# A first unit in a computed order, and later units with scores, transposes and value products at one place each

## The chip, the core and the metric

One core of a Trainium2 chip. The metric is device time in microseconds of one launch. Time before: 814.76 us, the median of 3 runs (812.94 to 815.05).

## The reference

Three stages in a chain, all in float32:

```python
scores = scale * q @ k.T                 # (4, 8, 576, 64): batch, heads, sequence, dim
# heads 0-3: keep 0 <= rel < 32;  heads 4-7: keep 0 <= rel < 128 and rel % 4 == 0
attn = exp(scores - max) / (sum + 1e-9)  # masked scores are -1e9
x = (attn @ v)  -> (2304 tokens, 512)
h = maximum(maximum(x @ w1, x @ w2), x @ w3);  x = h @ w_out           # 768 wide
h = x @ w_in;  g = P3(h) / (1 + |b0||h| + |b1|h*h + 1e-6);  out = g @ w_out   # 2048 wide
```

## The kernel before

**Tiling.** The 2304 tokens are cut into 12 chunks of 192; two chunks make a unit of 384 tokens, and there are 6 units. Per chunk the attention of the plain heads ("p") and of the dilated heads ("d", regrouped so that each residue modulo 4 is a dense band) goes through steps that have letters in the code: S (scores on TensorE, with the mask added by a TensorE matmul for chunks 0 to 3 and by VectorE after them), MX (row maximum, VectorE), E (exponentials, ScalarE; for chunks 0 to 3 one activation for each of 6 or 8 score blocks, with an accumulated sum, later one activation for all, with a subtraction before and a sum after it on VectorE), SB (division by the sum, VectorE), X (transposes on TensorE in two halves, each copied to SBUF), V (value products on TensorE) and VE (the split of the result into a rounded high part x1h on ScalarE and a remainder x1l on VectorE, both float32r).

**Split products.** Each product of the two later stages is three float32r matmuls (high by high, high by low, low by high), in the helper `mm3`, lines 494 to 499.

**The stage after attention** is `moe1(u)`: 18 groups h(f, j) of 12 matmuls of 384 columns (6 blocks f, 3 weights j, the maximum over j on VectorE) and 4 groups x(c) of 18 such matmuls. The weights arrive as raw 64-bit words and are converted in the kernel, one step at a time: load (SP queue), abs (ScalarE), bits (two VectorE instructions), hi (ScalarE), lo (VectorE). There are 24 of these tiles (18 of w1, w2, w3 and 6 of w_out), and `moe1(0)` needs each just as it comes to its group; the 32 tiles of the third stage are converted during units 1 to 4 and spread out over 88 slots.

**What sets the order.** The first unit's attention (chunks 0 and 1) is written out by hand in the string START and runs in that order on every queue. From line 630 a loop over the units issues `moe1(u)` group by group, and after each group one row of the string UNIT (UNIT0 for the chunks 2 and 3), which holds the attention steps of unit u + 1. In that loop a planner puts the instructions of each engine in order by when it reckons them ready, with priority to what was issued earlier; TensorE's order follows the rows. The loads of q, k, v and weights are all on SP's queue; stores of x2d and w2d are on POOL's. TensorE runs dummy matmuls at "W" words so that it isn't idle (helper `busy`).

**PSUM** has 8 banks: mm (3), sc (2), tp (1), pv (2). In UNIT a chunk's S:p and S:d stand 3 rows (5 in the second chunk) apart, its four transposes stand in rows of their own, all through the one tp bank, and V and VE of the second chunk stand in row 22, after the last group of the unit.

**The third stage** is untouched by the change: 6 tiles of 384 tokens by 16 slices, from about 405 us to the end.

Of the kernel before, what the change touches and what calls it, by code (L numbers as in the profile page):

```python
# [64 lines left out]

UNIT = """
-
Sa:p
-
MXa:p Ea:p  # L70
SBa:p Sa:d MXa:d Ea:d Xa:p,1
Xa:p,0 SBa:d
-
-
Xa:d,1 Va:p Xa:d,0
Va:d
VEa:d
-
Sb:p VEa:p
-  # L80
-
MXb:p
-
Eb:p SBb:p Sb:d MXb:d Xb:p,1
Eb:d
Xb:p,0
SBb:d Xb:d,0
Xb:d,1 Vb:p Vb:d VEb:d VEb:p
# [4 lines left out]
def kernel(  # L93
    ctx: ExitStack,
    tc: tile.TileContext,
    masks: bass.AP,
# [10 lines left out]
    a_co: bass.AP,  # L107
    b_co: bass.AP,
# [30 lines left out]
    ACT_UNITS = 4  # L139
    MASK_PE = 4  # L140
    SC_AT = {(0, "p"): "pv", (1, "p"): "mm", (1, "d"): "pv"}
    QA = 2
    CVT = 4
# [5 lines left out]
    AHEAD = 1  # L149
# [38 lines left out]
    at_k = {}  # L188
    x1 = {}

    def load_k(b, part=None):

        if b not in at_k:
            at_k[b] = (
                at.tile([128, 2, S], F32, tag="kTp", bufs=2, name=f"kTp{b}"),
                at.tile([128, 8, S // 4], F32, tag="kTd", bufs=2, name=f"kTd{b}"),
            )
        kTp, kTd = at_k[b]
        src = kp_in[b].rearrange("p (a t) -> p a t", a=2)
        if part is None:  # L200
            nc.sync.dma_start(out=kTp, in_=src)
        elif part == 0:
            nc.sync.dma_start(out=kTp[:, :, 0:CH], in_=src[:, :, 0:CH])
            return
        else:
            nc.sync.dma_start(out=kTp[:, :, CH:S], in_=src[:, :, CH:S])
            return
        nc.sync.dma_start(out=kTd.rearrange("p n m -> p (n m)"), in_=kd_in[b])

    def load_q(c, g):  # L210
        if c >= NCH:
            return
        if g == "p":
            t = at.tile([128, 2 * BP, 2 * QP], F32, tag="qTp", bufs=QA, name=f"qTp{c}")
            nc.sync.dma_start(out=t.rearrange("p n w -> p (n w)"), in_=qp_in[c])
        else:
            t = at.tile([128, 8, 2 * M], F32, tag="qTd", bufs=QA, name=f"qTd{c}")
            nc.sync.dma_start(out=t.rearrange("p n w -> p (n w)"), in_=qd_in[c])
        at_raw[c, g] = t
# [8 lines left out]
    def load_v(c):  # L228
        ci = c % NC
        vp = at.tile([WP, BP, NP, D], F32, tag="vp", name=f"vp{c}")  # L230
        nc.sync.dma_start(out=vp.rearrange("p i h d -> p (i h d)"), in_=vp_in[c])
        nm = dil(ci)[1]
        vd = at.tile([WD, NP, 4 * D], F32, tag="vd", name=f"vd{c}")
        nc.sync.dma_start(out=vd[:nm].rearrange("p h e -> p (h e)"), in_=vd_in[c, 0:nm, :])
        at_raw[c, "v"] = (vp, vd)

    def attn_pieces(c):
# [12 lines left out]
        def SC(g):  # L250
# [6 lines left out]
            for j in range(2):  # L257
                at_bank = SC_AT.get((c, g), "sc")
                if at_bank != "sc":
                    t = (mm_p if at_bank == "mm" else pv_p).tile(  # L260
                        [128, 512], F32, tag=at_bank, name="sc")
                else:
                    t = sc_p.tile([128, 512], F32, tag="sc", bufs=2, name="sc")
# [11 lines left out]
            m16, m32 = (mP16, mP32) if plain else (mD16, mD32)  # L275
# [4 lines left out]
            for n in range(U):  # L280
                i, blk = divmod(n, BP)
                if plain:
                    k0 = key0(ci, blk)
                    lq, rk = qT[:, n, :], kTp[:, i, k0:k0 + WP]
                else:
                    lq, rk = qT[:, n, :], kTd[:, n, m0:m0 + nmk]
                nc.tensor.matmul(scs[n // G][:, n % G, :], lhsT=lq, rhs=rk,  # L287
                                 start=not pem, stop=not pem or n % G == G - 1)
            load_q(c + QA, g)
            if g == "d" and ci == 0 and b + 1 < B:  # L290
                load_k(b + 1)
            sb = at.tile([Q, U, WP if plain else WD], F32, tag="s" + g, bufs=SBB, name="sb")
            mx = at.tile([Q, U, 1], F32, tag="mx" + g, bufs=2, name="mx")
            sm = at.tile([Q, U, 1], F32, tag="sm" + g, bufs=2, name="sm")
            grp[g] = (sb[:, :, :W], Q, W, U, sm, mx, scs, mask(m32))

        def MX(g):
# [11 lines left out]
            if c < ACT_UNITS:  # L309
                nc.vector.tensor_scalar_mul(mx, mx, -SCALE)  # L310

        def E(g):
            sv, Q, W, U, sm, mx, scs, mk = grp[g]
            G = U // 2
            if c < ACT_UNITS:
                for n in range(U):
                    src = scs[n // G][:, n % G, :] if c < MASK_PE else sv[:, n]
                    nc.scalar.activation(out=sv[:, n], in_=src, func=AF.Exp, scale=SCALE,
                                         bias=mx[:, n], accum_out=sm[:, n])
            else:  # L320
                nc.vector.tensor_tensor(out=sv, in0=sv, in1=mx.to_broadcast([Q, U, W]),
                                        op=ALU.subtract)
# [3 lines left out]
        def SB(g):  # L326
# [3 lines left out]
            nc.vector.tensor_tensor(out=sv, in0=sv, in1=sm.to_broadcast([Q, U, W]), op=ALU.mult)  # L330

        def X(g, j, dve=False, bank="tp"):
            sv, Q, W, U = grp[g][:4]
            G = U // 2
            if bank == "tp":
                tp = tp_p.tile([128, TU], F32, tag="tp", name="tpp")
            else:
                tp = sc_p.tile([128, 512], F32, tag="sc", bufs=2, name="tpp")[:, 0:TU]
            tp = tp[:W].rearrange("w (n q) -> w n q", q=Q)
            pt = at.tile([WP, TU], F32, tag="pt", bufs=PT, name="pt")[:W].rearrange(  # L340
                "w (n q) -> w n q", q=Q)
# [8 lines left out]
        def V(g):  # L350
            vp, vd = at_raw[c, "v"]
            if c == 0:
                pv = mm_p.tile([128, 512], F32, tag="mm", name="pv")
            else:
                pv = pv_p.tile([128, 512], F32, tag="pv", name="pv")
            pv = pv[:, 0:TU].rearrange("p (a t) -> p a t", a=2)
            for a in range(2):
                pt = pts["p", a] if g == "p" else None
                for n in range(BP if g == "p" else 4):
                    for j in range(2):  # L360
# [6 lines left out]
                        else:  # L367
                            pt = pts["d", j]
                            nc.tensor.matmul(pv[rows, a, M * n:M * n + M],  # L369
                                             lhsT=vd[:nmk, 2 * a + j, D * n:D * n + D],  # L370
                                             rhs=pt[:, 2 * (n // 2) + a,
                                                    M * (n % 2):M * (n % 2) + M],
# [3 lines left out]
        def VE(g):  # L376
            pv = grp["v" + g]
            if g == "p":
                src, dh, dl = pv, x1h[:, 0:2, tok], x1l[:, 0:2, tok]
            else:  # L380
                src = pv.rearrange("p a (r m) -> p a r m", r=4)
                dh = x1h[:, 2:4, tok].rearrange("p a (m r) -> p a r m", r=4)
                dl = x1l[:, 2:4, tok].rearrange("p a (m r) -> p a r m", r=4)
            nc.scalar.activation(out=dh, in_=src, func=AF.Copy)  # L384
            nc.vector.tensor_sub(dl, src, dh.bitcast(F32))  # L385
            if g == "d" and 0 < c < NCH - 1:
                load_v(c + 1)

        return {"S": SC, "MX": MX, "E": E, "SB": SB, "X": X, "V": V, "VE": VE}
# [11 lines left out]
    done_words = set()  # L401

    def attn(u):

        for row in (UNIT0 if u == 1 else UNIT).strip().split("\n"):
            for word in row.replace("-", "").split():
                word = word.replace("a:", f"{2 * u}:").replace("b:", f"{2 * u + 1}:")
                if word not in done_words:
                    do(word)
# [36 lines left out]
    def cv_abs(i):  # L446
# [27 lines left out]
    def cv_lo(i):  # L474
# [4 lines left out]
        else:  # L479
            nc.vector.tensor_sub(slot[:, 512:1024], t, slot[:, 0:512].bitcast(F32))  # L480

    cv_at = {"load": 0, "abs": 0, "bits": 0, "hi": 0, "lo": 0}
    cv_steps = (("hi", cv_hi, "bits"), ("lo", cv_lo, "bits"), ("abs", cv_abs, "load"),
                ("bits", cv_bits, "abs"), ("load", cv_load, None))

# [15 lines left out]

    def moe1(u):
        x1h, x1l = x1[u]
        hs = {}
        for f in range(F1):
            for j in range(3):
                ps = mm_p.tile([128, 512], F32, tag="mm", name="mm")
                o = ps[:, 0:TU]
                w = w1s[f, j]
                mm3(o, [(w[:, 128 * c:128 * c + 128], w[:, 512 + 128 * c:640 + 128 * c],  # L510
                         x1h[:, c, :], x1l[:, c, :]) for c in range(KC)])
                if j == 0:
                    t = com.tile([128, TU], F32, tag="m", bufs=MB, name="m")
                    nc.scalar.activation(out=t, in_=o, func=AF.Copy)
# [390 lines left out]
```

## Time and profile before

| | |
|---|---|
| median of 3 runs | 814.76 us |
| the profiled execution | 815.14 us, span 813.4 us |
| granted TensorE clock, mean | 0.991 |
| TensorE matmul busy | 800.1 us, 98% of the span |
| VectorE, ScalarE, GpSimd busy | 614.1, 487.9, 39.2 us |
| chain that ended last | 96% TensorE |
| DMA | 82.54 MB |

Times are microseconds from the first instruction. A busy time is the union of an engine's instructions; a matmul's recorded time is longer than its pitch, since matmuls overlap, so costs on TensorE are read from starts. The chain of waits is followed back from the last instruction; each piece's time there is the time by which it moved the end.

### The profile page before, as it was taken

The page shows a single profiled execution, that of the slowest core. Times are in us where ns is not written, and L with a number is a line of the kernel's source. Part 1 is how long each engine was busy: PE and PEld are TensorE (multiplying, and loading weights), DVE is VectorE, ACT ScalarE, POOL GpSimd, SP SyncE. Part 2 cuts the span into 40 slices and gives each one's busy share as a digit, 9 for nine tenths or more (in the row PEclk, how much of TensorE's full clock was granted, in tenths as well). Part 3 has the DMA queues.
Part 4 walks back from the last instruction along what each step waited for, and adds up shares of the span by engine and source line. Part 5 has one row for each costly group of instructions (what it writes and reads, how often), then busy time and mean ns, then how long its engine had stood idle before and what let it go on. Part 6 is the DMA issues. An engine that isn't in the chain of part 4 may idle for free.

```text
span 813.4 us, 13081 instructions
## 1 busy us (share of the span) xinstructions
PE 800.1 (98%) x4965; PEld 745.1 (92%) x4965; DVE 614.1 (76%) x1184; ACT 487.9 (60%) x1023; POOL 39.2 (5%) x77
## 2 busy tenths in 40 slices
PE   7899999999999999999999999999999999999998
PEld 5699999999999999999998899999999999999996
DVE  2679755655656646637389899999999999998996
ACT  3578623333333334245398887787778778777775
POOL 0000000110111110000000000000000000000000
PEclk9799999999999999999999999999999999999999
DMA  8677435754554544328310011010002001001001
GB/s 267 245 263 271 159 106 171 228 167 158 171 175 161 178 163 149 107 101 272 120 63 1 1 39 40 1 42 37 1 1 79 1 0 40 1 1 38 2 1 39
DMA packets 29438, 82.54 MB, mean 101 GB/s; under 512 B 3904, under 2 KB 7488, under 8 KB 29376
## 3 DMA queue, kind: packets, MB, share of 16 engines
q1 hardware_dynamic: 24080, 64.66, 24.7%
q0 software_dynamic: 5296, 17.04, 5.5%
q8 instruction: 39, 0.64, 0.3%
q14 instruction: 23, 0.19, 0.1%
HBM read 63.87 MB, written 17.83 MB: 100 GB/s over the span
## 4 chain that ended last, share of the span: by engine, by line
PE 96%; ACT 1%; DVE 1%; DMA 1%; issue 0%; SPq 0%; POOL 0%; ACTq 0%
PE mm L498 12%; PE mm L497 12%; PE mm L499 12%; PE h L498 8%; PE acc L769 8%; PE h L499 8%; PE h L497 8%; PE acc L767 8%; PE acc L768 8%; PE sc L287 4%; PE tpp L343 2%; PE pv L369 2%; PE pv L363 1%; DMA mk<-in_masks_dram 1%; ACT x1h L384 1%; PE warmth L604 0%
## 5 line engine op out<-in xcount | busy, mean ns | idle before, releaser
L497 PE MATMUL mm<-x1h,w1s 128*128 128x384 f32 x432 | 147.7, 343 | 0.0
L498 PE MATMUL mm<-x1l,w1s 128*128 128x384 f32 x432 | 146.0, 338 | 1.0 <-DVE x1l L385 1.0
L499 PE MATMUL mm<-x1h,w1s 128*128 128x384 f32 x432 | 145.2, 336 | 0.0
L498 PE MATMUL h<-x2l,w2s 128*128 128x384 f32 x384 | 129.2, 337 | 0.0
L499 PE MATMUL h<-x2h,w2s 128*128 128x384 f32 x384 | 129.0, 336 | 0.0
L497 PE MATMUL h<-x2h,w2s 128*128 128x384 f32 x384 | 128.9, 336 | 0.0
L767 PE MATMUL acc<-w2s,gh 128*128 128x512 f32 x288 | 113.6, 395 | 0.0
L768 PE MATMUL acc<-w2s,gh 128*128 128x512 f32 x288 | 113.4, 394 | 0.0
L769 PE MATMUL acc<-w2s,gl 128*128 128x512 f32 x288 | 109.8, 395 | 0.0
L718 ACT ACTIVATE q<-h 128x384 f32<-128x384 f32 x96 | 47.2, 491 | 76.1 <-PE h L499 75.5
L498 PEld LDWEIGHTS mm<-x1l,w1s 128*128 128x128 f32 x432 | 81.6, 189 | 2.2 <-DVE x1l L385 2.2
L497 PEld LDWEIGHTS mm<-x1h,w1s 128*128 128x128 f32 x432 | 81.3, 189 | 0.6
L499 PEld LDWEIGHTS mm<-x1h,w1s 128*128 128x128 f32 x432 | 81.6, 189 | 0.0
L497 PEld LDWEIGHTS h<-x2h,w2s 128*128 128x128 f32 x384 | 72.1, 188 | 3.9
L498 PEld LDWEIGHTS h<-x2l,w2s 128*128 128x128 f32 x384 | 72.0, 188 | 3.8
L499 PEld LDWEIGHTS h<-x2h,w2s 128*128 128x128 f32 x384 | 72.1, 188 | 0.3
L516 DVE TENSOR_TENSOR m<-mm,m 128x384 f32<-128x384 f32 x72 | 39.9, 554 | 42.2 <-PE mm L499 41.4
L725 DVE SCALAR_TENSOR_TENSOR q<-q,cs,ab 128x384 f32<-128x384 f32 x96 | 59.1, 615 | 15.5 <-ACT ab L719 15.4
L720 ACT ACTIVATE p<-h,cs 128x384 f32<-128x384 f32 x96 | 65.1, 678 | 0.0
L769 PEld LDWEIGHTS acc<-w2s,gl 128*128 128x128 f32 x288 | 54.1, 188 | 11.9
L768 PEld LDWEIGHTS acc<-w2s,gh 128*128 128x128 f32 x288 | 54.1, 188 | 9.4
L767 PEld LDWEIGHTS acc<-w2s,gh 128*128 128x128 f32 x288 | 54.0, 188 | 9.0
(86 smaller groups left out, 1471.8 us busy)
## 6 DMA issues: line engine op xcount, KB each, us to landing
w1r<-in_w_dram SPq DMA_DIRECT2D x18, 512.0 KB, 6.6
raw<-in_w_in_dram SPq DMA_DIRECT2D x16, 512.0 KB, 4.0
w2d<-cvt POOLq DMA_DIRECT2D x32, 256.0 KB, 2.6
raw<-in_w_out_dram SPq DMA_DIRECT2D x16, 512.0 KB, 3.6
w2r<-w2d SPq DMA_DIRECT2D x32, 256.0 KB, 3.6
qTp<-in_qp_dram SPq DMA_DIRECT2D x12, 384.0 KB, 4.1
qTd<-in_qd_dram SPq DMA_DIRECT2D x12, 384.0 KB, 4.5
x2d<-xs POOLq DMA_DIRECT2D x24, 192.0 KB, 2.5
```

What stands on the lines that cost most here:

```text
L287: nc.tensor.matmul(scs[n // G][:, n % G, :], lhsT=lq, rhs=rk, start=not pem, stop=not pem or n % G == G - 1)
L343: nc.tensor.transpose(tp[:, i, :], sv[:, G * j + i, :], ident[:Q, :Q])
L497: nc.tensor.matmul(o, lhsT=lh, rhs=rh, start=(i == 0), stop=False)
L498: nc.tensor.matmul(o, lhsT=lh, rhs=rl, start=False, stop=False)
L499: pe_at[0] = nc.tensor.matmul(o, lhsT=ll, rhs=rh, start=False, stop=(i == n - 1))
L516: nc.vector.tensor_tensor(out=t, in0=o, in1=t, op=ALU.max)
L718: nc.scalar.activation(out=s["q"], in_=s["h"], func=AF.Square)
L720: nc.scalar.activation(out=s["p"], in_=s["h"], func=AF.Identity, scale=cs[:, 3:4], bias=cs[:, 2:3])
L725: nc.vector.scalar_tensor_tensor(out=s["q"], in0=s["q"], scalar=cs[:, 5:6], in1=s["ab"], op0=ALU.mult, op1=ALU.add)
L767: nc.tensor.matmul(o, lhsT=gh, rhs=w[:, 0:512], start=(c == 0), stop=False)
L768: nc.tensor.matmul(o, lhsT=gh, rhs=w[:, 512:1024], start=False, stop=False)
L769: nc.tensor.matmul(o, lhsT=gl, rhs=w[:, 0:512], start=False, stop=(c == F2 - 1))
```

## The change

1. START now holds the whole of units 0 and 1's attention (chunks 0 to 3), the conversion of all 24 weight tiles and the whole of `moe1(0)`, in one written order; the loop begins at u = 1. `moe1` is cut into pieces for it: H:k and P:k are the groups (the first three in two halves of 192 tokens, H as soon as chunk 0's part is there), M the evictions and maxima, HH and HL the split, Y and YS the x groups.
2. The masks come as bfloat16, with the identity and the coefficients in one load; the casts on POOL and VectorE go. The warm-up matmuls have 128 columns and are put in four times the W number ahead of the next bank's first work.
3. For chunks 0 to 3 the exponentials come in three kinds (A: as before; B: subtraction on VectorE, one activation, sum on VectorE; C: one activation per block, sum on VectorE), and the division may go to ScalarE.
4. In UNIT S:p and S:d of a chunk stand in one row, the four transposes in one row (banks tp, sc, sc, pv), V:p and V:d in one row, and V of the second chunk one group earlier.
5. The tokens in a block of 64 are put in another order (host side: q rows, masks, output), so that the split of the dilated part writes contiguously; the value products of d write in pieces of 16.
6. Loads of q, k and v for later chunks (q from chunk 4, k from batch 2, v from chunk 4) go on POOL's queue.

```diff
 START = """
-W:7
-...
+qp0 kp0 mk L W:19 S0:p,mm qd0 kd0 up MX0:p bits L E0:p qd1 hi W:10 S0:d,mm SM0:p L up lo
+SB0:p,act MX0:d W:1 S1:d,sc qp1 D0:d bits kp1 E0:d X0:p,0,mm up X0:p,1,mm SM0:d v0 XC0:p,0 MX1:d
+XC0:p,1 SB0:d W:3 S1:p,mm E1:d bits v1 X0:d,0,tp MX1:p V0:p,pv XC0:d,0 SB1:d hi X0:d,1,sc L
+VH0:p D1:p W:1 X1:d,1,pv XC0:d,1 X1:d,0,tp XC1:d,1 VL0:p V0:d,mm L E1:p lo XC1:d,0 SM1:p L up
+V1:d,pv SB1:p VH0:d up L VL0:d X1:p,0,mm VH1:d X1:p,1,sc bits XC1:p,0 H:0 L XC1:p,1 VL1:d hi
+bits V1:p,mm L hi H:1 lo VH1:p qp2 VL1:p up lo hi P:0 k1 bits up S2:p,sc M:0 bits hi lo hi H:2
+...
+MX3:p E3:p Y:0 VH3:d SM3:p SB3:p VL3:d X3:p,1,tp YS:0 Y:1 XC3:p,1 X3:p,0,sc YS:1 Y:2 XC3:p,0,dve
+V3:p,mm YS:2 Y:3 VH3:p VL3:p YS:3
 """
 UNIT = """
-...
+-
+Sa:p Sa:d,pv
+MXa:p MXa:d
+Ea:p
+Ea:d SBa:p
+SBa:d
+-
+-
+Xa:p,0 Xa:p,1,sc Xa:d,0,sc Xa:d,1,pv
+-
+Va:p Va:d
+VEa:p VEa:d
+Sb:p Sb:d,pv
+MXb:p MXb:d
+Eb:p
+Eb:d SBb:p
+SBb:d
+-
+Xb:p,0 Xb:p,1,sc Xb:d,0,sc Xb:d,1,pv
+-
+Vb:p Vb:d
+VEb:p VEb:d
 """
+    EXPS = {"0:p": "C", "1:d": "A", "2:p": "A", "2:d": "A", "3:p": "C", "3:d": "C"}
-    CVT = 4
+    CVT = 3
+    def keep_warm(t):
+        for _ in range(4 * idle[0]):
+            nc.tensor.matmul(t[:, 384:512], lhsT=warm, rhs=warm, start=True, stop=True)
+        idle[0] = 0
+        return t
...
+        queue = nc.sync if c < 2 * QA else nc.gpsimd
...
+    def m1_mm(u, f, j, cols=slice(0, TU)):
+        if (u, f, j) not in m1:
+            m1[u, f, j] = bank("mm", "mm")[:, 0:TU]
+        x1h, x1l = x1[u]
+        w = w1s[f, j]
+        mm3(m1[u, f, j][:, cols], [(w[:, 128 * c:128 * c + 128], w[:, 512 + 128 * c:640 + 128 * c],
+                                    x1h[:, c, cols], x1l[:, c, cols]) for c in range(KC)])
...
+                elif op == "H":
+                    m1_mm(0, 0, int(arg), slice(0, CH))
+                elif op == "P":
+                    f, j = divmod(int(arg), 3)
+                    m1_mm(0, f, j, slice(CH if (0, f, j) in m1 else 0, TU))
...
+        for c in (4, 5):
+            for g in "pd":
+                load_q(c, g)
+        load_k(2)
...
-        for u in range(NU):
+        for u in range(1, NU):
```

Between the shown lines of START stand, in TensorE's order, P:1, P:2, S2:d, P:3 to P:6, X2:p (1), P:7, X2:p (0), P:8, S3:d, P:9, X2:d (1), P:10, X2:d (0), P:11, P:12, V2:p, P:13, V2:d, P:14, X3:d (0), P:15, X3:d (1), P:16, P:17, S3:p and V3:d, with the evictions and the conversions among them.

## Rows read from the trace of the kernel before

**Rows 1.** Busy time by stage: us and count of each engine, granted clock, DMA share, GB/s.
```profile
17.64:32.20 14.56, 11.27 (x122) 8.19 (x121) 11.48 (x31) 9.77 (x43) 0.00 (x0) 0.96 0.98 352
32.20:41.89 9.69, 9.69 (x82) 7.11 (x81) 3.95 (x9) 3.01 (x10) 0.00 (x0) 0.50 0.27 98
41.89:105.22 63.33, 63.33 (x469) 61.00 (x469) 50.26 (x104) 44.84 (x115) 1.76 (x3) 0.98 0.64 226
...
167.70:230.50 62.80, 62.56 (x485) 61.21 (x485) 37.30 (x73) 21.98 (x41) 7.01 (x13) 1.00 0.52 168
```

**Rows 2.** TensorE's timeline, first 45 us: start, us, line, operation, out<-in, count, idle before.
```profile
1.32 3.17 PE L604 MATMUL warmth<-warm 96*128 96x512 bf16 x7 [1.32 <-DVE cs L628]
8.19 0.66 PE L278 MATMUL sc<-mP,ident 128*128 128x288 bf16 x2 [3.70 <-POOL ident L582]
8.64 2.71 PE L287 MATMUL sc<-kTp,qTp 128*128 128x96 f32 x12
...
41.82 0.69 PE L497 MATMUL mm<-x1h,w1s 128*128 128x384 f32 x1
```

**Rows 3.** Busy time in steps of 2 us, columns as in the first group.
```profile
28.00:30.00 2.00, 0.27 (x2) 0.00 (x0) 1.23 (x2) 2.00 (x5) 0.00 (x0) 1.00 0.89 235
...
32.00:34.00 2.00, 1.80 (x13) 1.65 (x14) 0.53 (x2) 1.74 (x9) 0.00 (x0) 0.50 0.91 361
...
44.00:46.00 2.00, 2.00 (x11) 2.00 (x10) 1.97 (x6) 1.42 (x4) 0.00 (x0) 0.82 1.00 335
```

**Rows 4.** VectorE's instructions by line: shapes, count | busy us, mean ns | idle before.
```profile
L516 DVE TENSOR_TENSOR m<-mm,m 128x384 f32<-128x384 f32 x72 | 39.9, 554 | 42.2 <-PE mm L499 41.4 <-issue 0.5
L456 DVE TENSOR_SCALAR cvt<-cvt 128x512 int32<-128x512 int32 x56 | 23.3, 422 | 40.6 <-ACT cvt L450 40.6
...
L330 DVE TENSOR_TENSOR sb<-sb,sm 128x576 f32<-128x576 f32 (+2 forms) x24 | 17.9, 744 | 0.7
...
L302 DVE TENSOR_TENSOR sb<-sc,mk 128x288 f32<-128x288 f32 (+2 forms) x32 | 14.4, 453 | 4.5 <-PE sc L287 4.0
...
L480 DVE TENSOR_TENSOR w1s<-cvt,w1s 128x512 fp32r<-128x512 f32 x18 | 12.3, 681 | 0.0
L458 DVE SCALAR_TENSOR_TENSOR cvt<-w1r,cvt 128x512 int32<-128x512 int32 x18 | 12.2, 684 | 0.2
...
L324 DVE TENSOR_REDUCE sm<-sb 128x6 f32<-128x576 f32 (+2 forms) x16 | 12.0, 750 | 2.3 <-ACT sb L323 1.9
L307 DVE TENSOR_REDUCE mx<-sc 128x3 f32<-128x288 f32 (+2 forms) x16 | 6.7, 433 | 7.1 <-PE sc L287 7.0
```

**Rows 5.** Chain that ended last, unit 1: start, us, what.
```profile
109.54 1.31 PE sc L287 x12
...
117.15 1.34 PE sc L287 x16
118.49 0.33 PE tpp L343 x3
...
127.86 0.85 PE pv L363 x24
...
131.32 1.07 PE pv L369 x32
```

**Rows 6.** TensorE's timeline in unit 1, its first and its 24th matmul.
```profile
105.22 0.33 PE L497 MATMUL mm<-x1h,w1s 128*128 128x384 f32 x1
...
109.20 0.34 PE L499 MATMUL mm<-x1h,w1s 128*128 128x384 f32 x1
```

**Rows 7.** TensorE's timeline where unit 2 begins.
```profile
167.55 0.62 PE L497 MATMUL mm<-x1h,w1s 128*128 128x384 f32 x2
...
169.45 0.44 PE L498 MATMUL mm<-x1l,w1s 128*128 128x384 f32 x1 [0.24 <-DVE x1l L385]
```

**Rows 8.** VectorE's timeline at the same place.
```profile
167.22 0.56 DVE L385 TENSOR_TENSOR x1l<-pv,x1h 128x384 fp32r<-128x384 f32 x1 [2.58 <-ACT x1h L384]
168.54 0.85 DVE L385 TENSOR_TENSOR x1l<-pv,x1h 128x384 fp32r<-128x384 f32 x1 [0.76 <-ACT x1h L384]
```

More of the change, by code (lines that the diff above doesn't have):

```diff
@@ L95 @@
     tc: tile.TileContext,
-    masks: bass.AP,
+    consts: bass.AP,
     kp_in: bass.AP,
@@ L198, in load_k @@
         kTp, kTd = at_k[b]
[L199 to L208, printed above, removed]
+        queue = nc.sync if b < 2 else nc.gpsimd
+        for k, cut in ((0, slice(0, CH // 32)), (2, slice(CH // 32, S // 32))):
+            if part in (None, k):
+                queue.dma_start(out=kTp[:, cut].rearrange("p n a t -> p (n a t)"),
+                                in_=kp_in[b][:, 64 * cut.start:64 * cut.stop])
+        if part in (None, 1):
+            queue.dma_start(out=kTd.rearrange("p n m -> p (n m)"), in_=kd_in[b])
     def load_q(c, g):
@@ L368, in V, with split_of, VH, VL @@
                             pt = pts["d", j]
[L369 to L372, printed above, removed]
+                            at_n = pv[rows, a].rearrange("p (i r m) -> p r i m", r=4, m=16)[:, n]
+                            w_n = pt[:, 2 * (n // 2) + a, M * (n % 2):M * (n % 2) + M]
+                            nc.tensor.matmul(at_n, lhsT=vd[:nmk, 2 * a + j, D * n:D * n + D],
+                                             rhs=w_n.rearrange("w (i m) -> w i m", m=16),
                                              start=True, stop=True)
             grp["v" + g] = pv
-        def VE(g):
+        def split_of(g):
             pv = grp["v" + g]
[L378 to L383, printed above, removed]
+            at_p = slice(0, 2) if g == "p" else slice(2, 4)
+            return pv, x1h[:, at_p, tok], x1l[:, at_p, tok]
+        def VH(g):
+            src, dh, _ = split_of(g)
             nc.scalar.activation(out=dh, in_=src, func=AF.Copy)
+        def VL(g):
+            src, dh, dl = split_of(g)
             nc.vector.tensor_sub(dl, src, dh.bitcast(F32))
-            if g == "d" and 0 < c < NCH - 1:
+            done_v[c] = done_v.get(c, 0) + 1
+            if done_v[c] == 2 and c > 2:
                 load_v(c + 1)
-        return {"S": SC, "MX": MX, "E": E, "SB": SB, "X": X, "V": V, "VE": VE}
+        return {"S": SC, "MX": MX, "D": DF, "E": E, "SM": SM, "SB": SB, "X": X, "XC": XC,
+                "V": V, "VH": VH, "VL": VL}
     at_fn = {}
@@ L399, in do @@
         at_fn[c][name](*[x if x.isalpha() else int(x) for x in arg.split(",")])
-    done_words = set()
+    parts = {"E": ("D", "E", "SM"), "X": ("X", "XC"), "VE": ("VH", "VL")}
     def attn(u):
-        for row in (UNIT0 if u == 1 else UNIT).strip().split("\n"):
+        for row in UNIT.strip().split("\n"):
+            late = []
             for word in row.replace("-", "").split():
-                word = word.replace("a:", f"{2 * u}:").replace("b:", f"{2 * u + 1}:")
-                if word not in done_words:
-                    do(word)
+                op, _, arg = word.partition(":")
+                for part in parts.get(op[:-1], (op[:-1],)):
+                    step = f"{part}{2 * u + (op[-1] == 'b')}:{arg}"
+                    if part == "XC":
+                        late.append(step)
+                    else:
+                        do(step)
+            for step in late:
+                do(step)
             yield
@@ L596, in cv_step @@
             cv_at[name] += 1
-        def busy(n, bank="mm"):
-            if bank == "mm":
-                t = mm_p.tile([128, 512], F32, tag="mm", name="warmth")
-            else:
-                t = sc_p.tile([128, 512], F32, tag="sc", bufs=2, name="warmth")
-            for _ in range(n):
-                nc.tensor.matmul(t, lhsT=warm[:, 0:128], rhs=warm[:, 0:512], start=True, stop=True)
         with tc.manual_schedule():
@@ L609 @@
                 if op == "L":
-                    for _ in range(int(arg)):
-                        cv_step("load")
-                elif op == "v":
-                    load_v(int(arg))
+                    cv_step("load")
+                elif op in loads:
+                    loads[op]()
                 elif op == "W":
-                    busy(*[x if x.isalpha() else int(x) for x in arg.split(",")])
+                    idle[0] = int(arg)
+                elif op == "H":
[3 more added lines that the diff above has]
+                    m1_mm(0, f, j, slice(CH if (0, f, j) in m1 else 0, TU))
+                elif op == "M":
+                    m1_max(0, *divmod(int(arg), 3))
+                elif op in ("HH", "HL", "Y", "YS"):
+                    {"HH": m1_hh, "HL": m1_hl, "Y": m1_y, "YS": m1_ys}[op](0, int(arg))
                 elif op in steps:
@@ L619 @@
                     do(word)
-                    done_words.add(word)
         cs = const.tile([128, 8], F32, name="cs")
@@ L661 @@
                 slot += 1
-                if u == 0:
-                    pass
-                elif not last:
+                if not last:
                     tick += 1
```

331 lines of the change are left out of this document (167 added, 164 removed).

## The prediction

> **What bounds the kernel now.** I read the table of stages first. From 41.89 us on TensorE is busy without a break in each stage (63.33 of 63.33, 62.56 of 62.80), and before that it is not the bound: in 17.64 to 32.20 it works 11.27 of 14.56 us, VectorE 11.48, ScalarE 9.77, so a chain through three engines sets the pace, and in 32.20 to 41.89 the granted clock is 0.50 [rows 1]. TensorE's timeline of the start says the same in starts: the first scores at 8.19 us, after 3.70 us of waiting, and the first matmul of the second stage only at 41.82 [rows 2]. The 33 us between hold the attention of two chunks, which at full speed is some 12 us of TensorE's work (below). That is the first place to gain. The second is small: the chain of waits for a later unit shows what each piece costs [rows 5], and the sum of the pieces is a little less than the unit's period. The third stage isn't touched by the change.
>
> **Prices.** A matmul of 384 columns has a pitch of (109.20 - 105.22) / 23 = 0.173 us [rows 6], so a `moe1` of 18 x 12 + 4 x 18 = 288 takes 49.8 us. A chunk's attention on TensorE is 1.31 + 1.34 + 4 x 0.33 + 0.85 + 1.07 = 5.9 us [rows 5]. Two mask matmuls took 0.66 us at the start [rows 2], where 12 scores took 2.71 us against 1.31 later [rows 5], that is half speed; so 0.3 us a pair, 0.6 us a chunk.
>
> **Part 1: the start up to the first group.** The masks no longer pass through a cast, and S0:p can start some 0.4 us earlier; this is small. What counts is when H:0, the first half group, can start. It needs chunk 0's split (VH0, VL0 of both kinds) and stands on TensorE behind both chunks' scores, all eight transposes and three of the four value products. I take VectorE's list, since it was the busiest in that stretch. Ahead of H:0 it has four conversions' bits at 0.42 + 0.68 = 1.1 (4.4), two lo at 0.68 (1.4), eight maxima at 0.43 (3.5), four subtractions at 0.45 (1.8), three sums at 0.75 (2.3), three divisions at 0.74 with two small instructions (an estimate of 0.35 for both; 3.3, and 0.35 for the fourth, whose product goes to ScalarE), and two splits at 0.55 (1.1): 18.1 us [rows 4], the split from [rows 8]. It starts when the first half of S0:p is there: 8.19 - 0.4 and half of the mask and score time of [rows 2], which gives 9.5 at half speed and 8.6 at full speed; I take 9.3. Never idle, it would be done at 27.4; its instructions overlap a little in the record, which gives back some 2 us, and it will idle for latencies, as it did for 3.1 of 14.56 us [rows 1]. I set these against each other: H:0 at 27.5. The bounds are 25 (overlap given back, no idling) and 36 (chained as badly as before: 41.82 less the 4.8 us that 9.69 busy us at half clock lost [rows 1, 2], and less about 1 for casts and first scores; rival 2).
>
> **Part 2: from H:0 to the end of `moe1(0)`.** In the new order what TensorE has left is 49.8 of `moe1(0)`, 0.85 for V1:p, and two chunks with masks at 6.5: 63.7 us. That is about the 63.33 us in which the old kernel did the same work with TensorE always busy [rows 1], so conversions can be hidden there: VectorE needed 50.26 and ScalarE 44.84 of those 63.33 us. VectorE's work doesn't grow as a whole: the sums and subtractions that come onto it for the new kinds of exponential (five sums at 0.75, four subtractions at 0.45) are 5.6 us, four products that go to ScalarE and two fewer copies take off about 4. As four of 24 tiles are begun before H:0, VectorE is needed for less than 50 us of the 63.7. The tail is tight: between S3:p and X3:p,1 TensorE has only V3:d and Y:0 (1.07 + 18 x 0.173 = 4.2 us) to cover maximum, sum and division on VectorE (0.9 + 0.75 + 1.1 = 2.8 [rows 4]) and six exponentials on ScalarE between them; I count 0.5 us lost. For clock and waits I put 1.5 us more. The halves: 72 matmuls of 192 columns take the place of 36. No row shows one; at half of 0.173 they cost nothing more, at the 2.71 / 12 / 2 = 0.11 us of a 96-column score at full speed 72 x (0.11 - 0.087) = 1.7 us, and if they paid per column what that score pays (0.22 us each), 9.6 us. I take 1.7, the row nearest in weights (128 x 128 loaded). So `moe1(0)` ends at 27.5 + 63.7 + 2.0 + 1.7 = 94.9 against 105.2 [rows 6]: **-10.3 us**. Bounds: 25 + 63.7 = 88.7 (-16.5) and 36 + 63.7 + 2 + 9.6 = 111 (+6).
>
> **Part 3: later units (u = 1 to 4).** From 167.55 [rows 7] the period is 62.8 us [rows 1]; the pieces make 49.8 + 2 x 5.9 = 61.6. Of the 1.2 us between, about 0.5 is lost where a unit begins: eight matmuls (1.4 us) fill the 1.9 us from 167.55 to 169.45, and the ninth waits for x1l [rows 7], whose strided split runs at 168.54 for 0.85 us [rows 8]. With V one group earlier and the split contiguous (0.55 instead of 0.85), a group of 3.1 us lies over it, and the wait goes. The other 0.7 us belongs to ten changes between stage and attention, 0.07 each; six are left, and 0.3 us goes. 0.8 x 4 = **-3.2 us**. The bound on the one side is the whole 1.2 x 4 = 4.8; on the other side stands rival 3. What is late next: from S to X there are now 5 groups of 2.08, one of 3.1 and S:d's 1.34, 14.9 us, in the second chunk. VectorE has to do there, for a chunk of 80-key blocks, four mask sums at 0.45, and six passes of 0.75 (two maxima, two sums, two products) and two subtractions of the same size, with small ones 8.5 us; six maxima or splits of the stage at 0.55, 3.3; and 36 x 6 / 88 = 2.5 conversions at 1.1, 2.7: 14.5 of 14.9 [rows 4]. It fits, and the conversions have the lowest priority; but there is no room. Value products in pieces of 16 and keys in blocks of 32 have no row; the same number of columns streams, and I take nothing. Loads on POOL: its busy time is 7.01 of 62.80 us [rows 1], ten more issues cost POOL some 6 us, and they are for data needed 30 us later. If that cover went, a chunk would wait for a load.
>
> **Sum.** -10.3 - 3.2 = -13.5 against the profiled execution's 815.14: 801.6. That execution is 0.4 us above the median of the runs, so I say **801.2**.
>
> [...]
>
> **Rivals.**
> 1. *The clock falls again.* TensorE still idles in the start, and in the old run a half-clock stretch of some 12.4 us (from about 32 to 44.7, by the 0.82) followed such idling [rows 3]. If it falls on the dense stream, 6.2 us are lost in place of the 1.5 counted: 805.9. For it: the chain from S to V is no shorter for the last chunk. Against: TensorE's list up to H:0 is 15 us with its dummies in 18. Chance 0.15.
> 2. *The start doesn't shrink.* The chain of three engines keeps its old idling and conversions get in the way: H:0 at 36, 8.5 us later: 809.7. For it: ScalarE gets a division by the sum and its conversions into the same stretch. Chance 0.12.
> 3. *Slower: one place for all four transposes.* They wait in TensorE's own order until both divisions are done, and everything behind them waits too. At 14.5 of 14.9 us a few conversions run ahead of a division (1.1 each) are enough. There are 8 such places; from 13.5 / 8 = 1.7 us each the gain is gone, at 3 us each 24 us are lost and the time is 801.2 + 24 = 825. Against: the order is planned with conversions last, and the first chunk of a unit has one group more. Chance 0.08.
> 4. *Weights come late.* By the last of the 24 tiles about 20.6 MB have to be loaded (24 x 0.52 for weights, 8 x 0.39 for q, 2.4 for k, 2.2 for v, 0.3 for the constants); at the 226 GB/s of the old stage [rows 1] this is done at 91 us plus the start's 2, and the last Y would wait some 3 us: 804. At the 352 GB/s of 17.64 to 32.20 [rows 1] nothing waits. Chance 0.05.
>
> **How the numbers follow.** Forecast 0.60 (its own range 796 to 806), rivals 0.15, 0.12, 0.08, 0.05. The range 793.5 to 811 takes in the low bounds of parts 1 and 3 (-16.5 - 4.8, 793.4) and rivals 1, 2 and 4; what lies outside is rival 3, and the dear halves together with a late start. A change under 0.3% (2.4 us) can't be told from none here. Faster by more: 0.60 + 0.15 + 0.05 and most of rival 2, 0.88; within 0.04; slower 0.08.
>
> **What would show it.** Right: the first x1h matmul on TensorE before 30 us; the first matmul of unit 1 at 92 to 97 us; periods of unit 1 to 4 of 62.0 us with no wait for x1l; granted clock 1.00 after 30 us. Wrong: waits of transposes for VectorE's product in the units (rival 3), a row at 0.50 after 30 us (rival 1), first half groups with starts more than 0.15 us apart (the dear halves), waits of the conversions for loads (rival 4).

## The result and the profile after

The changed kernel took 803.73 us (median of 4 runs, 801.25 to 807.42), the kernel before 814.62 beside it: a ratio of 0.9868 [0.9842, 0.9894]. In a second series (a1_again) it took 800.55 (6 runs, 798.08 to 804.93), 0.9834 [0.9808, 0.9861]. The forecast of 801.2 was right in the total. It was not right in its terms: the start gave 3.9 us less than forecast, and the third stage, whose code the change doesn't touch, gave 3.6 that nobody had forecast.

TensorE's timeline of the start, changed kernel (start, us, line, operation, out<-in, count, idle before); it answers to [rows 2]:

```profile
0.99 7.22 PE L180 MATMUL sc<-warm 128*128 128x128 bf16 x76 [0.99 <-DVE warm L631]
8.05 0.41 PE L285 MATMUL sc<-mk 128*128 128x288 bf16 x2
8.30 1.47 PE L297 MATMUL sc<-kTp,qTp 128*128 128x96 f32 x12
...
18.70 1.55 PE L297 MATMUL sc<-kTp,qTp 128*128 128x96 f32 x12 [1.46 <-DMA kTp<-in_kp_dram]
...
29.37 0.51 PE L544 MATMUL mm<-x1h,w1s 128*128 128x192 f32 x1
...
32.81 0.27 PE L544 MATMUL mm<-x1h,w1s 128*128 128x192 f32 x1
32.92 0.28 PE L545 MATMUL mm<-x1l,w1s 128*128 128x192 f32 x1
```

The first scores run at full speed (12 in 1.47 us, before 2.71), chunk 1's scores wait for their keys, and the first matmul on x1h comes at 29.37 instead of 41.82. The halves come 0.11 us apart. The windows of that stretch (columns as in [rows 1]) show the clock at half from inside 20 to 22 us to inside 30 to 32:

```profile
16.00:18.00 2.00, 1.06 (x14) 0.59 (x11) 1.89 (x7) 1.70 (x6) 0.00 (x0) 1.00 1.06 207
18.00:20.00 2.00, 1.30 (x12) 1.33 (x13) 1.86 (x4) 2.00 (x14) 0.00 (x0) 1.00 1.04 183
20.00:22.00 2.00, 2.00 (x32) 1.73 (x31) 1.72 (x6) 1.14 (x4) 0.00 (x0) 0.64 1.02 218
22.00:24.00 2.00, 2.00 (x17) 1.99 (x16) 1.77 (x4) 1.06 (x3) 0.00 (x0) 0.50 1.01 354
...
30.00:32.00 2.00, 2.00 (x25) 1.90 (x26) 1.16 (x2) 1.34 (x3) 0.00 (x0) 0.80 1.06 406
```

TensorE worked 1.06 and 1.30 of 2 us ahead of the fall. The DMA engines were busy throughout, at 183 to 218 GB/s; the keys' load was under way for 11.84 us by the chain of waits:

```profile
6.72 11.84 DMA kTp<-in_kp_dram
```

The units begin here (TensorE's timeline, the first matmul on x1h of units 1 to 5), and the third stage runs between the two rows behind them:

```profile
98.80 0.33 PE L544 MATMUL mm<-x1h,w1s 128*128 128x384 f32 x1
...
160.14 0.33 PE L544 MATMUL mm<-x1h,w1s 128*128 128x384 f32 x1
...
222.31 0.33 PE L544 MATMUL mm<-x1h,w1s 128*128 128x384 f32 x1
...
284.49 0.33 PE L544 MATMUL mm<-x1h,w1s 128*128 128x384 f32 x1
...
346.52 0.33 PE L544 MATMUL mm<-x1h,w1s 128*128 128x384 f32 x1
...
396.83 0.33 PE L544 MATMUL h<-x2h,w2s 128*128 128x384 f32 x1
...
795.27 0.39 PE L825 MATMUL acc<-w2s,gl 128*128 128x512 f32 x1
```

The same of before, with unit 5 at 356.42:

```profile
105.22 0.33 PE L497 MATMUL mm<-x1h,w1s 128*128 128x384 f32 x1
...
406.99 0.34 PE L497 MATMUL h<-x2h,w2s 128*128 128x384 f32 x1
...
808.98 0.39 PE L769 MATMUL acc<-w2s,gl 128*128 128x512 f32 x1
```

| part | before | after | gained | forecast |
|---|---|---|---|---|
| to the first matmul on x1h | 41.82 | 29.37 | 12.45 | 14.3 |
| from there to unit 1 | 63.40 | 69.43 | -6.03 | -4.0 |
| units 1 to 4 | 251.20 | 247.72 | 3.48 | 3.2 |
| unit 5 | 50.57 | 50.31 | 0.26 | 0 |
| third stage | 401.99 | 398.44 | 3.55 | 0 |
| all | | | 13.71 | 13.5 |

The waits of TensorE from 9 us to the end are three, all in the first unit; the waits for x1l where a unit begins [rows 7] are gone, and none for VectorE's division has come:

```profile
PE sc L297 <- DMA kTp<-in_kp_dram: 1.5, 1, 1.5
PE tpp L376 <- ACT pt L387: 0.4, 1, 0.4
PE sc L285 <- ACT pt L387: 0.2, 1, 0.2
```

### The profile page after: what moved, and what is told of

Read it like the earlier page. It is cut to its first block, busy times and chain, and to the rows that moved or that the text cites. A ratio compares the mean times of both kernels' runs of the same rounds, so it can differ in the third digit from the quotient of the medians.

```text
span 799.5 us, 13370 instructions
## 1 busy us (share of the span) xinstructions
PE 792.4 (99%) x5108; PEld 749.4 (94%) x5108; DVE 606.7 (76%) x1184; ACT 484.4 (61%) x1007; POOL 59.1 (7%) x113
## 4 chain that ended last, share of the span: by engine, by line
PE 92%; DMA 3%; DVE 2%; ACT 2%; SPq 1%; issue 0%; ACTq 0%
PE mm L544 12%; PE mm L545 11%; PE mm L546 11%; PE h L546 8%; PE h L544 8%; PE h L545 8%; PE acc L824 8%; PE acc L823 8%; PE acc L825 8%; PE sc L297 3%; PE tpp L376 2%; PE pv L407 2%; DMA kTp<-in_kp_dram 1%; PE pv L399 1%; DMA x2r<-x2d 1%; DMA raw<-in_w_in_dram 1%
## 5 line engine op out<-in xcount | busy, mean ns | idle before, releaser
L544 PE MATMUL mm<-x1h,w1s 128*128 128x384 f32 (+1 forms) x444 | 150.0, 338 | 0.1
L546 PE MATMUL mm<-x1h,w1s 128*128 128x384 f32 (+1 forms) x444 | 147.4, 332 | 0.0
L545 PE MATMUL mm<-x1l,w1s 128*128 128x384 f32 (+1 forms) x444 | 147.3, 332 | 0.0
L825 PE MATMUL acc<-w2s,gl 128*128 128x512 f32 x288 | 108.1, 389 | 0.0
L544 PEld LDWEIGHTS mm<-x1h,w1s 128*128 128x128 f32 x444 | 83.9, 189 | 0.9 <-ACT m L563 0.4
L545 PEld LDWEIGHTS mm<-x1l,w1s 128*128 128x128 f32 x444 | 83.8, 189 | 0.0
L546 PEld LDWEIGHTS mm<-x1h,w1s 128*128 128x128 f32 x444 | 83.7, 189 | 0.0
L503 DVE TENSOR_SCALAR cvt<-cvt 128x512 int32<-128x512 int32 x56 | 23.6, 422 | 61.3 <-ACT cvt L497 61.1
L823 PEld LDWEIGHTS acc<-w2s,gh 128*128 128x128 f32 x288 | 54.0, 188 | 8.6
```

The lines of the kernel that those rows point to most:

```text
L503: nc.vector.tensor_scalar(out=t, in0=t, scalar1=3, scalar2=None, op0=ALU.logical_shift_left)
L544: nc.tensor.matmul(o, lhsT=lh, rhs=rh, start=(i == 0), stop=False)
L545: nc.tensor.matmul(o, lhsT=lh, rhs=rl, start=False, stop=False)
L546: pe_at[0] = nc.tensor.matmul(o, lhsT=ll, rhs=rh, start=False, stop=(i == n - 1))
L823: nc.tensor.matmul(o, lhsT=gh, rhs=w[:, 0:512], start=(c == 0), stop=False)
L825: nc.tensor.matmul(o, lhsT=gl, rhs=w[:, 0:512], start=False, stop=(c == F2 - 1))
```

## The experiments

**The start and the units.** a1_again is the changed kernel as it is. a2_old_units:

```diff
-UNIT: the new rows                       +UNIT: the rows of before
-late.append(step)   # copies last        +do(step)   # each copy behind its transposes
```

a3_fill_gap puts 28 more dummies ahead of chunk 1's scores, and a4_no_warm drops every W word, 136 dummies:

```diff
-XC0:p,1 SB0:d W:3 S1:p,mm E1:d ...
+XC0:p,1 SB0:d W:10 S1:p,mm E1:d ...
```

Expected:

> The changed kernel once more, nothing altered. Two questions. (1) Its executions came at 801.25, 801.25, 806.21 and 807.42 us with mean granted clocks of 0.993, 0.997, 0.989 and 0.986. Theory: the longer ones have a longer stretch at half clock in the start or the dense stream behind it; then times and clocks go together again, and executions with a clock of 0.99 or less are the ones near 806. Rival: they have nothing to do with the clock; then long executions come at high clocks too. (2) In the profiled execution the 512-column matmuls of the third stage, which the change does not touch, had a pitch of about 229 ns against 233 before (3.6 us over 864). Theory: this belongs to the kernel (where its tiles lie) and comes again at 229. Rival: it belongs to the execution and may come at 233.

> The changed kernel with the rows of the old UNIT (scores, transposes and value products of a chunk spread out, the last value products in row 22, copies right behind their transposes), the new start kept. Theory: the units 1 to 4 get the wait at their end back, without the strided split (about 0.4 us each), and ten changes between stage and attention instead of six (0.07 to 0.1 each): 2.5 to 3.5 us slower than the changed kernel, periods of 62.7 us. Rival (the new rows bring nothing by themselves, the contiguous split does it all): the same time, periods of 62.1.

> 28 more dummy matmuls ahead of S1:p (the word W:3 becomes W:10), which fill most of the 2.4 us in which TensorE waits for the keys of the chunks behind the first (16.3 to 18.7 us). Theory: the fall of the clock at 20.7 us follows from the idle time at 16 to 20; with it filled the clock stays up, the first half group starts 1.5 to 3 us earlier, and the time is 1 to 3 us lower and less scattered. Rival: VectorE and ScalarE set the start of the first half group, or the clock falls all the same: no change, or up to 1 us slower.

> All dummy matmuls of the start taken out (136). Theory: the first scores run at half speed as in the old kernel, and the chain behind them; the first half group starts 3 to 6 us later, and the time is 3 to 8 us higher. Rival: the loads of keys set the pace in the start, so the dummies are idle decoration: within 1 us.

Measured: a1 800.55 (798.08 to 804.93, mean clock of the executions 0.986 to 1.000); a2 803.55 (801.36 to 803.97); a3 798.21 (797.77 to 799.22, clock 0.998 or more); a4 801.83 (798.95 to 804.63).

*a3.* The fall of the clock goes with the changed kernel's long executions, as a1's first theory said: of its ten, the four with a mean clock of 0.989 or less took 804.70 to 807.42 us, the six with 0.993 or more 798.08 to 801.25. The dummies hold the clock up: the nine executions of a3 and of its repetition d2 have 0.997 or more. TensorE's timeline and windows of a3:

```profile
15.00 2.40 PE L180 MATMUL sc<-warm 128*128 128x128 bf16 x40
...
18.48 1.55 PE L297 MATMUL sc<-kTp,qTp 128*128 128x96 f32 x12 [0.83 <-DMA kTp<-in_kp_dram]
...
26.10 0.33 PE L544 MATMUL mm<-x1h,w1s 128*128 128x192 f32 x1
...
95.93 0.33 PE L544 MATMUL mm<-x1h,w1s 128*128 128x384 f32 x1
```

```profile
16.00:20.00 4.00, 3.17 (x42) 2.89 (x39) 2.55 (x8) 2.56 (x16) 0.00 (x0) 1.00 1.05 197
20.00:24.00 4.00, 3.87 (x81) 3.29 (x80) 3.87 (x9) 3.21 (x7) 0.00 (x0) 1.00 1.01 317
24.00:28.00 4.00, 3.50 (x63) 3.28 (x63) 3.83 (x10) 3.28 (x7) 0.00 (x0) 1.00 1.02 407
```

Chunk 1's scores start where they did (18.48 against 18.70), since the keys land no sooner; but from there to unit 1 it is 77.45 us instead of 80.10. So the fall cost 2.65 us in this execution. In the profiled a1 the keys landed later, the clock stayed at 1.00, and from the scores to unit 1 it was 77.72:

```profile
20.57 1.55 PE L297 MATMUL sc<-kTp,qTp 128*128 128x96 f32 x12 [2.53 <-DMA kTp<-in_kp_dram]
```

An idle time of 2.5 us alone thus did not decide whether the clock fell. Three other profiled runs with the same start (a2, and b1 and e1 below) had the fall too, and it cost more the longer it lasted: from the scores to unit 1 it took 81.47 us in a2 and 81.65 in e1, with some 13.7 us at half clock, and 86.26 in b1, with some 23.9 (some 10.2 in the changed kernel's first profile).

*a4.* That the dummies of the first 8 us are worth several us is refuted: without any, the first matmul on x1h comes at 26.84 and the time stands within the spread of a1 (the medians are 1.3 us apart, so the rival's "within 1 us" isn't shown either). TensorE's timeline of a4:

```profile
5.96 0.66 PE L285 MATMUL sc<-mk 128*128 128x288 bf16 x2 [5.96 <-DMA mk<-in_consts_dram]
6.41 2.71 PE L297 MATMUL sc<-kTp,qTp 128*128 128x96 f32 x12
```

The scores run at half speed but start at 6.41 instead of 8.30: the 76 dummies of the changed kernel end at 8.05, though VectorE has the constants at 5.54. They win 1.24 us on the twelve scores (1.47 against 2.71) and delay them by 1.89.

*a2.* Units 2 to 4 take 62.33, 62.46 and 62.44 us with the old rows, against 62.17, 62.18 and 62.03 with the new ones and 62.88, 63.02 and 62.97 before; all of units 1 to 4 249.53, 247.72 and 251.20. So the rows are 1.8 us of the gain, 1.0 of it in unit 1. The 0.85 us in units 2 to 4 are firm: all eleven traces with the new rows have 62.17, 62.18 and 62.03 there. Unit 1 is not: it takes 60.67 to 64.31 us in them (61.34 in the middle), against 62.30 to 62.33 in the three with the old rows. The rest, 0.55 us in each unit from the second on, is the wait for x1l, and that is gone in a2 too: VectorE's second split there takes 0.56 us instead of the 0.85 of [rows 8]; of the changes that a2 keeps, the new order of the tokens is the one that touches this instruction. So a2's theory, that the wait comes back, failed, and its rival, that the rows bring nothing, failed too. The 3.0 us between the medians of a2 and a1 aren't the rows' alone, since the profiled a2 had the fall of the clock.

```profile
224.76 0.56 DVE L423 TENSOR_TENSOR x1l<-pv,x1h 128x384 fp32r<-128x384 f32 x1 [0.40 <-ACT x1h L419]
```

**The third stage, the keys, the halves.** In all five profiles taken up to then of kernels with the new start, the third stage took 398.4 us. Its matmuls of 512 columns are the same in code and number. Their tiles are opened behind the pool of constants, which is 1,184 bytes per partition smaller in the changed kernel.

```diff
+pad = pad_pool.tile([128, 296], F32)    # b1: in the changed kernel, ahead of w2c and wk
+pad = pad_pool.tile([128, 728], F32)    # b2: in the kernel before, at the same place
 w2c = ...   # the last nine weights
 wk = ...    # q, ab, p, r, gh, gl, ob
```

> The changed kernel with 1,184 bytes per partition left empty ahead of the third stage's tiles, so that these lie at the addresses that they have in the kernel before; one memset of a column is the only instruction added. Theory, the third stage's 3.5 us come from where its tiles lie (after has a smaller pool of constants, so all tiles opened behind it lie 1,184 bytes lower): the 512-column matmuls come 233 ns apart instead of 229, the third stage takes 402.0 us instead of 398.4, and the time is 804 us against 800.6 for the changed kernel. Rival, they come from something else in the changed kernel (its queues, its instruction stream): 229 ns, 398.4 us, 800.6 us.

> The kernel before with 2,912 bytes per partition left empty ahead of the third stage's tiles, so that these lie exactly 4,096 bytes above where the changed kernel has them. Theory, placement decides (by an address's place within 4,096 bytes or less): 229 ns between 512-column matmuls instead of 233, a third stage of 398.4 us instead of 402.0, the whole kernel at 811.5 us, 0.4% faster than the kernel before, with nothing else changed. Rival, not placement: 402.0 us and no difference.

Measured, TensorE's first and last matmul of the third stage in b1 and in b2:

```profile
402.79 0.33 PE L544 MATMUL h<-x2h,w2s 128*128 128x384 f32 x1
...
804.81 0.39 PE L828 MATMUL acc<-w2s,gl 128*128 128x512 f32 x1
```

```profile
407.69 0.34 PE L497 MATMUL h<-x2h,w2s 128*128 128x384 f32 x1
...
806.11 0.39 PE L772 MATMUL acc<-w2s,gl 128*128 128x512 f32 x1
```

402.02 and 398.42 us: placement decides, in both directions. The kernel before with 2,912 unused bytes took 810.95 us, 0.9954 [0.994, 0.9968] of itself without them, with no other change. b1 took 802.81 (801.55 to 810.81; the longest is the profiled one, with the long fall of the clock named above).

b3_keys_first and, after its result, c1_keys_up bring chunk 1's queries and keys ahead of two weights on SP's queue:

```diff
-... up MX0:p bits L E0:p qd1 hi W:10 S0:d,mm SM0:p L up lo ... S1:d,sc qp1 D0:d bits kp1 ...
+... up MX0:p bits E0:p qd1 hi W:10 S0:d,mm qp1 kp1 SM0:p L lo ... S1:d,sc v0 D0:d L ...
 b3: the second weight's "up" stays ahead of XC0:p; c1: "up", "bits", "hi" of weights 2 and 3 behind the copies of X0
```

> The changed kernel with two loads of weights (512 KB each) moved behind the queries, keys and values of chunk 1 and chunk 0 in SyncE's order, and what reads those weights moved behind too; no dummies added. Theory, the order of the loads paces the first 27 us: chunk 1's first scores begin by 16 us instead of 18.5 to 20.6, there is no wait for the keys there and no fall of the clock, the first matmul on x1h comes at 23.5 to 25 us against 26.1 in the kernel with the gap filled, and the time is 795 to 797 us. Rival, the rate of the transfers paces it whatever their order: what is won at the keys is lost at the values or at the second weight, the first matmul on x1h comes at 26 us or later, 798 to 801 us.

> The order of loads of b3_keys_first again, with what converts the second and third weight moved behind the copies of the transposed probabilities on ScalarE (in b3 ScalarE stood for 2.5 us at the second weight, which landed at 18.1 us, ahead of those copies, and VectorE 1.6 us behind it). Theory, keys and queries of chunk 1 do pace the start, and b3 lost only by what stood behind the weight in ScalarE's order: chunk 1's first scores begin at 15.5 to 16.5 us, no wait of over 0.5 us there, the clock stays up, the first matmul on x1h comes at 23.3 to 25 us, 795 to 797.5 us. Rival, the start is bound by the transfers as a whole (409 GB/s while they run, 0.2 to 0.25 of a us per 64 KB when values are among them): the wait moves to the values or to the second weight, the first matmul on x1h comes no earlier than 26 us, 798 us or more.

Both theories failed: 803.19 (802.87 to 803.42) and 804.02 us (803.1 to 805.5). The first matmul on x1h came at 31.97 us in b3 and at 28.21 in c1. In b3 ScalarE, which works in the written order, stood at the second weight's load, with the copies of the transposes behind it; TensorE waited for one of them, and the clock fell there (0.96 in the window from 18 to 20 us, 0.50 from 20 to 32), so that b3 does not tell what each of the two cost. ScalarE's timeline, and TensorE's:

```profile
18.12 0.66 ACT L497 ACTIVATE cvt<-w1r 128x512 f32<-128x512 f32 x1 [2.51 <-DMA w1r<-in_w_dram]
18.68 0.85 ACT L387 ACTIVATE pt<-tpp 96x384 f32<-96x384 f32 x2
```

```profile
19.21 0.28 PE L285 MATMUL sc<-mk 128*128 128x288 bf16 x1 [2.78 <-ACT pt L387]
```

In c1 chunk 1's scores did start at 15.98 us, 2.5 us before a3's, with no wait for keys. Then ScalarE and VectorE were late; TensorE waited 1.54 us for a copy by the one and 1.65 for a division by the other:

```profile
15.98 1.47 PE L297 MATMUL sc<-kTp,qTp 128*128 128x96 f32 x12
...
27.04 1.52 PE L376 MATMUL tpp<-mk,spare 128*96 128x128 f32 x6 [1.65 <-DVE spare L365]
28.21 0.51 PE L544 MATMUL mm<-x1h,w1s 128*128 128x192 f32 x1
```

And the clock fell behind these waits:

```profile
28.00:32.00 4.00, 4.00 (x33) 3.82 (x33) 2.61 (x5) 1.97 (x4) 0.00 (x0) 0.50 1.03 402
```

Unit 1 began at 102.20 us in c1, 6.27 later than in a3: 2.11 of it arose ahead of the first matmul on x1h and 4.16 behind it, where the clock stood at half until inside 36 to 40 us. c1 with dummies in its waits was not run.

So the keys are one of two limits that lie close together. Behind them, as far as these traces show, is VectorE: in a3 it works 7.70 of the 8 us from 20 to 28 (the windows above), and in c1 a conversion that I had put there stood on VectorE in front of chunk 1's division, by the chain of waits:

```profile
24.73 0.44 DVE cvt L503
25.20 0.69 DVE cvt L505
...
26.23 0.77 DVE spare L365
```

Whether an order exists that gains from the earlier keys was not found out.

b4_whole is a3 without the halves (H:0 to H:2 dropped, P:0 to P:2 whole); d1_whole_warm holds the clock in it, with d2_fill_again, a3 once more, beside it:

```diff
-VL0:d X1:p,0,mm ... bits V1:p,mm ... hi P:0
+VL0:d W:2 X1:p,0,mm ... bits W:2 V1:p,mm ... hi W:2 P:0
```

> The kernel with the gap filled (798.2 us), and its three groups of 192-column halves done as whole 384-column groups once chunk 1 is there: 36 matmuls fewer, 1.7 us by 72 x 0.111 against 36 x 0.1735. Theory, the halves pay because they are work that TensorE has while chunk 1 is not ready (8 us of them): without them TensorE waits 3 to 6 us ahead of the first group and the time is 799.5 to 802.5 us. Rival, the chain of chunk 1 comes that much earlier by itself when nothing stands in its way: a wait of under 1.7 us, 797 to 798.2 us.

> b4_whole (the gap ahead of chunk 1's scores filled, no halves) with eight more dummies in each of its three waits of 0.5 to 0.6 us at 25.5, 27.0 and 29.1 us. In b4 the granted clock fell behind the first of them, at 26.8 us, and stood at half until 33.3 us. Theory, b4 has lost to the clock what it saved by doing the groups whole: with the clock up, its first matmul on x1h comes at 28.5 to 29.5 us, unit 1 starts at 94.3 to 95.5 (97.3 in b4, 95.9 with halves), and the time is 796 to 797.5 us, so that the halves, at 192 columns in 0.111 us against 384 in 0.174, buy nothing once the gap is filled. Rival, the halves do pay: the dummies don't hold the clock or VectorE sets the pace there anyway, unit 1 starts at 95.9 or later, 798 to 800 us.

> The kernel with the gap filled a second time, to stand beside d1_whole_warm on the same chip: 797.8 to 799.2 us, unit 1 at 95.9 us and no fall of the clock if the filling holds whatever the execution; over 800 us in some of its executions if it held by luck.

b4 took 799.07 (798.28 to 800.48), between what its theory (799.5 to 802.5) and its rival (797 to 798.2) said. TensorE did not wait the theory's 3 to 6 us ahead of the first group, but three times 0.5 to 0.6 us; among these waits the clock fell:

```profile
26.00:27.00 1.00, 0.92 (x6) 0.60 (x6) 0.96 (x3) 0.97 (x3) 0.00 (x0) 0.82 1.02 406
```

With the clock held (1.00 in all four windows from 16 to 32 us of the profiled execution), d1 took 797.42 (796.66 to 800.07), and unit 1 began at 95.19, within its theory's 94.3 to 95.5:

```profile
28.88 0.45 PE L544 MATMUL mm<-x1h,w1s 128*128 128x384 f32 x1 [0.29 <-ACT x1h L419]
...
95.19 0.33 PE L544 MATMUL mm<-x1h,w1s 128*128 128x384 f32 x1
```

d2 took 798.38 (797.18 to 801.47), so d1 and d2 can't be told apart by their times. The halves buy nothing once the gap is filled; their use was to keep TensorE at work. The profiled d2, 801.47 us, shows another source of spread: in unit 1 ScalarE stood at a raw weight of the third stage. VectorE's next step for that weight waited for it, with a maximum behind it, and the split hh, which needs this maximum, came late. ScalarE's timeline, TensorE's, and the window after it:

```profile
142.47 0.66 ACT L497 ACTIVATE cvt<-raw 128x512 f32<-128x512 f32 x1 [4.60 <-DMA raw<-in_w_in_dram]
```

```profile
145.39 0.44 PE L544 MATMUL mm<-hh,wo1s 128*128 128x384 f32 x1 [1.34 <-ACT hh L569]
```

```profile
148.00:150.00 2.00, 2.00 (x9) 2.00 (x8) 0.43 (x1) 1.38 (x3) 0.02 (x1) 0.50 0.26 98
```

Unit 1 took 64.31 us there against 61.52 in a3.

**Last: which tiles.** e1_pad_wk puts the 1,184 bytes between w2c and wk, so that only the work tiles move:

```diff
 w2c = ...
+pad = pad_pool.tile([128, 296], F32)
 wk = ...
```

> The changed kernel with the 1,184 bytes left empty between the third stage's last weights and its work tiles (q, ab, p, r, gh, gl, ob), so that the work tiles lie where the kernel before has them and the weights w2s stay where the changed kernel has them. Theory, the work tiles decide (gh and gl are what the 512-column matmuls load as stationary operand): 233 ns, a third stage of 402.0 us, 804 us. Rival, the weights decide (w2s is what these matmuls stream): 229 ns, 398.4 us, 800.6 us.

```profile
398.72 0.33 PE L544 MATMUL h<-x2h,w2s 128*128 128x384 f32 x1
...
800.83 0.40 PE L828 MATMUL acc<-w2s,gl 128*128 128x512 f32 x1
```

402.11 us, 802.38 in all (800.91 to 806.8): moving the work tiles alone brings back the whole difference. The weights alone were not moved. With the work tiles there, the weights' place doesn't change the sum, but in e1 the 512-column matmuls come 234.1 ns apart and those of 384 columns 173.9, against 232.8 and 174.7 in b1. Of the work tiles the matmuls load gh and gl; whether it is their place or that of the tiles which ScalarE and VectorE read and write meanwhile stays open.

## Why the prediction was right, and where it was not

**To the first half group: 27.5 forecast, 29.37 measured.** VectorE's list was a sound measure: a3 has 26.10 and a1 28.20, and in a3 VectorE was busy for 15.47 of the 18.24 us from its first maximum to that matmul, near the list's 18.1 less 2 for overlap. What it left out is a load. I checked conversions and weights for late loads, but not chunk 1's keys, which stand behind three weights on SP's queue; they landed at 18.56 us, and TensorE idled for 1.46 us there. Rival 1 then took part of its price, but ahead of the dense stream rather than in it: 2.65 us by a3 against the 4.7 given to it. In b1, with the same start, it took more than its price: 8.8 us against a3 (86.26 less 77.45), with the clock at half until inside 40 to 44 us, well into the dense stream. The old stretch that rival 1 was priced by was also read a little short: the clock fell inside 30 to 32 us (0.77 in that window), so it lasted some 13.7 us, not 12.4.

**From there to unit 1: 67.4 forecast, 69.43 measured.** This is the step that failed by size. The halves cost what I took: 0.111 us apart, against 0.087 for half of a whole one. The allowance of 1.5 us for clock and waits was too small. Behind an attention piece the first whole matmul is followed after 0.256 to 0.281 us instead of 0.174, ten times, and two halves are late in the same way: 1.0 us. I had counted such changes for the later units (0.07 each) and none here. The half clock left 0.7 on the first halves, the wait for a copy with its tail 0.6, two changes to value products 0.2. Attention took 14.4 us instead of 13.85, and the 72 matmuls of Y 13.0 instead of 12.5 (the 252 on x1h and x1l took the other 42.0, all from start to start). Together this is 3.5 of the 4.0 us above the 63.7 + 1.7 of work, against the 2.0 allowed for clock, waits and tail. The stall forecast at X3:p did not come. By its own signs the prediction missed here as well: unit 1 began at 98.80 us, not at 92 to 97, and the clock was at half until inside 30 to 32 us.

**Later units: right, and for the reasons given.** 3.48 against 3.2. By a2 the wait for x1l is 0.55 us a unit (0.5 forecast) and the rows with their fewer changes 0.2 to 0.4 in units 2 to 4 (0.3 forecast). The fourth wait for x1l stood at the start of unit 5 (50.57 us before, 50.05 in a2), where the forecast had none, and unit 1, which had none, gained 1.0. The run a2 also sharpens the first reason: the contiguous split alone ends the wait, and V one group earlier wasn't needed for it. Rival 3 did not come: no transposes waited for VectorE in units 1 to 4, though I had counted 14.5 of 14.9 us there.

**Third stage: "isn't touched" was wrong.** It is not touched in code, but its tiles moved. This gave 3.55 us and hid the two errors above: without it the profiled execution would have been 804.8.

**The first scores.** They ran at full speed, 12 in 1.47 us against 2.71 before; part 1 took a start for VectorE between the two speeds. No time was won by that: against a4 the dummies ahead of them delay the same scores by 1.89 us and speed them by 1.24.

**The spread.** 801.2 was 0.05 us from the profiled execution, by luck; ten executions of this kernel lie between 798.1 and 807.4. What moves them, as far as the traces show, is when the keys land (scores at 18.0 to 20.6 us in five traces with this start), whether the clock falls there and for how long (not at all in a1, some 10 to 24 us in the other four), and, by d2, late weights in unit 1.

The best versions are a3_fill_gap (798.21, ratio 0.9792 [0.9779, 0.9806]; 798.38 and 0.9805 [0.9779, 0.9831] the second time) and d1_whole_warm (797.42, 0.9802 [0.9777, 0.9827]).

## What to carry to other kernels

When an order is computed anew, list for each operation at the start the load that it needs and its place in the queue: with an idle gap of 1.46 us the fall of the clock cost 2.65 more (8.8 in b1, with a gap of 2.92), and 28 dummies in the gap held the clock up (0.997 or more in nine executions), while the 76 dummies in front of the first scores delayed them by 1.89 us against a4 and shortened them by 1.24. An engine that works in written order must not meet a late load ahead of what others wait for; b3 lost its gain in that way, with 2.78 us of waiting on TensorE, together with the fall of the clock behind it (0.50 from 20 to 32 us). And if a stage that nobody edited changes its time (3.55 us here), compare where its tiles lie before looking for a cause in its schedule.

## What the runs showed that was not expected

- A shift of the work tiles by 1,184 bytes per partition changes 864 matmuls of 512 columns by 3.55 / 864 = 4.1 ns each (some 233 against 229 ns), at 398.4 to 398.5 us of the stage in eleven traces with the one place (in b2 4,096 bytes above it) and 402.0 to 402.1 in three with the other.
- Matmuls of 192 columns with 128 x 128 weights came 0.111 us apart, of 384 columns 0.174: half the columns for 64% of the time.
- The granted clock fell after TensorE had worked 2.36 of 4 us (16 to 20 us of the changed kernel), and did not fall in a1, where it idled for 2.53 us at one place.
